# Queries stored with contiguous weight columns and their zeros in place, one load per unit

## The chip, the cores and the metric

The kernel runs on one core of a Trainium2 chip. The metric is the device time of an execution in microseconds (us). The core has engines with queues of their own: TensorE (PE, with PEld for its weight loads), VectorE (DVE), ScalarE (ACT), GpSimd (POOL), and SyncE (SP), which issues the DMAs here. Each engine runs its instructions in the order in which the program gives them.

## The reference

Local attention followed by a two-layer network with a rational activation. Cut to what matters:

```python
# q, k, v: [8 batches, 8 heads, 576 positions, 64]
scores = (1/8) * q @ k.T                 # per batch and head
# heads 0-3: keys 0..31 positions back; heads 4-7: 0..127 back, every fourth
attn = softmax(where(mask, scores, -1e9))
x = (attn @ v), heads side by side       # [4608 tokens, 512]
h = x @ w_in                             # [4608, 2048]
g = (a0 + a1 h + a2 h^2 + a3 h^3) / (1 + |b0| |h| + |b1| h^2 + 1e-6)
out = g @ w_out                          # [4608, 512]
```

All of it in float32; the weights arrive as float64 or float32.

## The kernel before

**Attention.** Heads 4 to 7 have their positions sorted by residue modulo 4, so that all heads attend to a window of 32 positions. The work of a batch is cut into six *units* (`NU = 6`, 48 in all). A unit is six blocks of 32 queries for each of four heads: two pairs of heads (`h` = 0, 1), each pair with an even and an odd head (`e` = 0, 1). The 64 dimensions of the even head lie on partitions 0 to 63 and those of the odd head on 64 to 127.

One matmul makes the scores of one block of 32 queries of *both* heads of a pair. The 64 columns of its weights (the stationary operand) are 32 columns of the even head and 32 of the odd one. For the two heads not to mix, the even head's columns are zero on the partitions of the odd head, and the other way round. The tile `q` of a unit is thus 128 x 768 floats, half of them zeros. In DRAM (`qk`) the queries lie without zeros, 384 columns for 128 partitions, beside the keys.

- `zero_halves` and `zero_q` (L232, L245) set the zeros with two memsets of 64 x 384. Each of the six units of batch 0 (the *start*) has a `q` tile of its own in a slot of a weight that comes late, and memsets of its own; the other 42 units share one tile, `q_keep`, whose zeros are set once and stay.
- `load_q` (L241) loads a unit's queries with two DMAs, one for each half of the partitions.
- `scores` (L260) reads the tile as `(h m j)`: the six blocks `j` are innermost, so that the 64 columns `m` of one matmul's weights lie six floats apart. Twelve matmuls make a unit's scores; each shows as two weight loads and two matmuls in the trace. From batch 1 on, the two pairs `h`, whose results go to different halves of the PSUM partitions, take turns; in batch 0 the blocks of one pair come before those of the other. In batch 1 the masks are added by twelve small matmuls more.

After the scores (`s_ps`, PSUM) come mask, maximum, exponential, sum and normalization on DVE, ACT and POOL; then the scores are turned, by PE for batches 0 to 2 and mostly by DVE transposes of 32 x 32 blocks (`turn`, L328) later; then the product with `v` (`av`, `o_ps`), and the split of its result into a high and a low part (`xh`, `xl`), since the network's matmuls take float32r operands.

**The network.** Tokens are cut into nine chunks of 512. The first eight hold the first 512 tokens of each batch, the last one what is left (`x_left`). For each chunk there are 16 *tiles* of 128 hidden features, 144 in all. A tile is 12 matmuls `h`, a rational function on ACT, DVE and POOL (`r`, `a`, `t`, `gh`, `gl`), and 12 matmuls `out`. A chunk's tiles can only start once its batch's attention is done; the attention of the batches after it runs beside the tiles, about a batch for every 16 tiles. The weights are converted in the first part of the run (`wi_f`, `wo_f`, `wi`, `wo`).

**The order.** `Plan` (L62) is a list scheduler in the program that builds the kernel. Each operation has a modelled time on one of some engines, a rank (when it is due), dependences and buffers; among those that can start next on an engine, the lowest rank is taken. The order that comes out is the order of each engine's queue on the chip. For the score step the planner has 972 ns (1045 in batch 0); for the load of `q`, 120 ns of SP and 196608 bytes. In the start the load of `q` follows its memsets.

Of the kernel before, what the change touches and what calls it, by code (L numbers as in the profile page):

```python
# [8 lines left out]
F32 = mybir.dt.float32  # L9
# [7 lines left out]
B, H, S, D = 8, 8, 576, 64  # L17
NT, DM, DFF = B * S, 512, 2048
P = 128
# [3 lines left out]
NU = 6  # L23
# [3 lines left out]
# Periods of a batch from which on its units are due.  # L27
DUE = (-1.58, 1.49, 3.34, 6.42, 8.91, 12.25)
# Tiles whose operations' ranks come from when they are due.
# [5 lines left out]
# Mask blocks over a 32-query x 64-key window: 0 all keys within the window,  # L35
# 1 the segment starts at the block, 2 at its query 16, 3 at query 16 of the block before.
STRIP = [1, 0, 0, 0, 2, 3]
# For each unit of a batch: (first block, blocks, place in STRIP, or None where all are 0).
# [11 lines left out]
class Op:  # L50
    """An operation of one of some engines (engine: ns). With a slack, its rank follows from when
    those that depend on it are due, or from the period `by` which it has to be done."""
# [8 lines left out]
class Plan:  # L61
    """List schedule: an operation starts when its engine, what it depends on and the  # L62
    buffers it takes are free; of those that can start next, the lowest rank does."""
# [6 lines left out]
    def op(self, engs, rank, fn, *deps, dma=0):  # L70
        o = Op(engs, rank, fn, deps, dma)
        self.ops.append(o)
        return o

    def takes(self, o, tag, bufs, users):
        """o takes a buffer of a tag, which is free again after its users."""
        self.tags.setdefault(tag, (bufs, []))
        o.takes.append((tag, users))

    def due(self):  # L80
        """Ranks of operations with a slack."""
        after = {}
        for o in self.ops:
            for d in o.deps:
                after.setdefault(id(d), []).append(o)
        seen = set()

        def rank(o):
            if o.slack is None or id(o) in seen:
                return o.rank  # L90
            seen.add(id(o))
            ns = min(o.engs.values()) + self.HOP
            if o.dma:
                ns += self.DMA_NS + o.dma / self.DMA_RATE
            due = [rank(n) for n in after.get(id(o), [])] + ([] if o.by is None else [o.by])
            o.rank = min(due) - ns / self.PERIOD - o.slack
            return o.rank

        for o in reversed(self.ops):
            rank(o)  # L100
# [50 lines left out]
def tile_attention_moe(  # L151
# [10 lines left out]
    nc = tc.nc  # L162
# [5 lines left out]
    att = ctx.enter_context(tc.tile_pool(name="att", bufs=1))  # L168
    psum = ctx.enter_context(tc.tile_pool(name="psum", bufs=1, space=bass.MemoryType.PSUM))

    # Every engine runs its instructions in the order in which they are written,
    # which a list schedule of the operations below settles.
    pin = tc.keep_in_program_order
    plan = Plan()
    op = plan.op

    def load(dst, src):
        pin(nc.sync.dma_start(dst, src))  # L178
# [33 lines left out]
    NQ, NKEY, NV = 2 * 6 * 32, 2 * 224, 3 * 2 * 2 * 64  # L212
    xT = {}

    def x_slot(c):
        # chunk 0's second part comes after chunk 1
        return "0" if c == 0 or (c > 2 and c % 2) else "1"
# [9 lines left out]
    def halves(q):  # L227
        # for each half of the partitions (a head of each pair): the columns of either head
        q = q.rearrange("p (h e c) -> p e h c", h=2, e=2)
        return [[q[64 * e : 64 * e + 64, c] for c in range(2)] for e in range(2)]  # L230

    def zero_halves(eng, q):  # L232
        for e, half in enumerate(halves(q)):
            pin((nc.gpsimd if eng == "POOL" else nc.vector).memset(half[1 - e], 0.0))

    class Unit:
        def __init__(self, b, u):
            self.b, self.u, self.n = b, u, b * NU + u
            self.q = q_keep

        def load_q(self):  # L241
            for e, half in enumerate(halves(self.q)):
                load(half[e], qk[self.n, 64 * e : 64 * e + 64, :NQ].rearrange("p (h c) -> p h c", h=2))

        def zero_q(self, eng, pool, tag):  # L245
            self.q = pool.tile([P, 2 * NQ], F32, tag=tag, name=f"q{self.n}")
            zero_halves(eng, self.q)
# [12 lines left out]
        def scores(self, tag, masked):  # L260
            q_t = self.q.rearrange("p (h m j) -> p h j m", h=2, j=6)
            k_t = self.k.rearrange("p (h k) -> p h k", h=2)
            self.s = ps = self.bank(tag, "s_ps")
            pairs = [(h, j) for j in range(6) for h in range(2)]
            # alternate halves of the partitions take turns in the array
            for h, j in pairs if self.b else sorted(pairs):
                cols = slice(64 * j, 64 * j + 64)
                if masked:
                    mm(ps[64 * h : 64 * h + 64, cols], ident_b[:, :64] if h == 0 else ident_b[:, 64:], mask_t[:, BLOCKS[self.u][j]], stop=False)
                mm(ps[64 * h : 64 * h + 64, cols], q_t[:, h, j, :], k_t[:, h, 32 * j : 32 * j + 64], start=not masked)  # L270
# [57 lines left out]
        def turn(self, h, e):  # L328
            # 32 x 32 blocks of this head's scores, each to the partitions of its keys
            src = self.p[64 * h + 32 * e : 64 * h + 32 * e + 32].rearrange("p (i par) k -> p par i k", par=2)  # L330
            for par in range(2):
                for kh in range(2):
                    row = 64 * par + 32 * kh
                    pin(nc.vector.transpose(self.pT[row : row + 32, :, h, e, 32 * par : 32 * par + 32], src[:, par, :, 32 * kh : 32 * kh + 32]))  # L334
# [10 lines left out]
        def pieces(self):  # L345
            """(columns of the result, tokens of the chunk) of this unit, and those left for the last chunk"""
# [39 lines left out]
        def plan(self, p, start):  # L386
            """p: the period from which on this unit is due; start: buffers of the start, or None"""
# [6 lines left out]
            # where each step runs  # L394
# [5 lines left out]
            # Loads run ahead, in the order of need.  # L400
            l_rank = p - 4
            lq = op({"SP": 120}, l_rank, lambda e: self.load_q(), dma=NQ * 512)
            zq = op({"POOL": 720, "DVE": 600}, -90 + u, lambda e: self.zero_q(e, qp, qt)) if start else q_zeroed
            lq.follows.append(zq)
            lk = op({"SP": 60}, l_rank + 0.01, lambda e: self.load_k(kp, kt), dma=NKEY * 512)
            lv = op({"SP": 60}, l_rank + 2.02, lambda e: self.load_v(vpool, vt), dma=NV * 512)
            sc = op({"PE": (972 if b else 1045) + 180 * on_pe}, p - 4.97, lambda e: self.scores(s_tag, on_pe), zq, lq, lk, *([masked, identity] if on_pe else []))
# [26 lines left out]
            # the order of units, and of those that share the bank of the attention  # L434
# [23 lines left out]
            for tag, o, users in ((qt, zq if start else lq, [sc]), (kt, lk, [sc]), (vt, lv, [av])):  # L458
                plan.takes(o, tag, 1, users)
# [31 lines left out]
    def w_scale(key):  # L491
        # float64: the high word as a float32 holds sign, exponent / 8 and the mantissa's start.
        # Times 2^-112 its bits are float32's exponent and 20 mantissa bits, three places low.
        wf[key] = w = work.tile([P, 512], F32, tag="stage", name="%s_f%d" % key, bufs=4)
        act(w, w_words(key)[:, :, 1].bitcast(F32), AF.Abs, scale=2.0**-112)
# [48 lines left out]
    spare_x = {}  # L544

    def spares(part):
        # The last tiles of all have the slot of x that the last chunk doesn't take.
        if part not in spare_x:
            slot = "01"[x_slot(NC - 1) == "0"]
            spare_x[part] = xpool.tile([P, NK, 512], F32 if part == "h" else F32R, tag="x" + part + slot, name="spare_" + part)  # L550
        return spare_x[part]

    class Tile:
        def __init__(self, i, c, ft, first, last):
            self.i, self.c, self.ft, self.first, self.last = i, c, ft, first, last
            # place among the last three tiles
# [112 lines left out]
    # The first part of chunk 0's sums waits in DRAM.  # L669
# [17 lines left out]
    # Zero but for its blocks of keys and queries; the start has another, in a slot of a late weight.  # L687
# [24 lines left out]
    q_keep = att.tile([P, 2 * NQ], F32, tag="q", name="q_keep")  # L712
    q_zeroed = op({"POOL": 720, "DVE": 600}, -60, lambda e: zero_halves(e, q_keep))
# [5 lines left out]
    keys = sorted([("wi", n) for n in range(NF)] + [("wo", n) for n in range(NF)], key=lambda x: x[1] + 1.5 * (x[0] == "wo"))  # L719
    for u in range(NU):  # L720
        start = {
            # banks of out before its first product, and slots of weights that come late
# [44 lines left out]
    # Loads are issued in the order of their ranks until the weights are there.  # L767
# [65 lines left out]
```

## Time and profile before

| what | value |
|---|---|
| median of 3 runs | 993.52 us (992.5 to 993.93) |
| span of the profiled execution (first to last instruction) | 991.2 us; its own device time is not recorded apart from the span |
| busy PE, PEld | 939.3 us, 759.9 us |
| busy DVE, ACT, POOL | 884.7, 683.8, 497.3 us |
| mean granted TensorE clock | 0.993 |
| DMA | 68.80 MB, mean 69 GB/s |
| score matmuls | 1152, of them 144 in batch 0 |
| loads of `q` | 96, of 96 KB each |

A row of a group of instructions gives the line, the engine, the operation, output <- inputs, their shapes and the count, then after a bar the busy time in us and the mean of one in ns, and after the next bar the idle time of that engine just before them with what ended it. A row of waits reads: who waited <- for whom: us in total, times, the longest. In rows of stretches and of the timeline times count from the start of the span. Most matmul lines carry the line number of a helper (L181), so that the names of the tiles tell them apart.

### The profile page before, as it was taken

What the parts mean: (1) busy time and instruction counts of PE and PEld (TensorE: products, weight loads), DVE (VectorE), ACT (ScalarE), POOL (GpSimd) and SP (SyncE); (2) the same over time, 40 slices, a digit from 0 to 9 for tenths busy, and PEclk for the clock granted to TensorE, in tenths of its full rate; (3) what the DMA queues carried; (4) which work ended last, traced back from release to release, by engine and by line L of the source; (5) the groups of instructions that cost most, each with busy time, mean ns of one, the idle gap of its engine ahead of it and who ended that gap; (6) DMA issues with size and microseconds to landing.
All of it is one profiled execution on the core that took longest, in us unless ns stands there. A gap on an engine that the chain in (4) does not pass through costs nothing.

```text
span 991.2 us, 16536 instructions
## 1 busy us (share of the span) xinstructions
PE 939.3 (95%) x5883; PEld 759.9 (77%) x5883; DVE 884.7 (89%) x1747; ACT 683.8 (69%) x1146; POOL 497.3 (50%) x422
## 2 busy tenths in 40 slices
PE   6698898989999999999999999999999999999998
PEld 6576676667887787877877888788877778888886
DVE  6999999999899999999999999999999986656565
ACT  2787877666656666766676667666776678778776
POOL 3676677885544444443544444344443445454443
PEclk9989999999999999999999999999999999999999
DMA  8734910003331111312121122121221001001001
GB/s 257 254 105 132 385 63 1 19 16 107 104 97 55 52 50 34 109 34 68 34 76 56 46 66 77 34 67 35 60 84 39 28 1 43 1 1 43 1 1 42
DMA packets 38962, 68.80 MB, mean 69 GB/s; under 512 B 4448, under 2 KB 23008, under 8 KB 38880
## 3 DMA queue, kind: packets, MB, share of 16 engines
q1 hardware_dynamic: 38736, 67.65, 21.2%
q8 instruction: 46, 0.75, 0.3%
q14 instruction: 36, 0.29, 0.1%
q0 software_dynamic: 144, 0.10, 0.1%
HBM read 57.35 MB, written 10.49 MB: 68 GB/s over the span
## 4 chain that ended last, share of the span: by engine, by line
DVE 49%; PE 41%; issue 4%; DMA 2%; SPq 1%; ACT 1%; DVEq 0%; ACTq 0%
PE h L181 19%; PE out L181 18%; DVE h L190 10%; DVE a L190 10%; DVE p_T L334 9%; DVE t L187 4%; PE s_ps L181 3%; DVE wo_f L190 2%; DVE sm L310 2%; DVE wi_f L190 2%; DVE xl L187 2%; DVE p L187 2%; SPq L178 1%; DVE sm L307 1%; PE o_ps L181 1%
## 5 line engine op out<-in xcount | busy, mean ns | idle before, releaser
L181 PE MATMUL h<-xh,wi 128*128 128x512 f32 x1152 | 386.2, 396 | 21.8 <-DVE a L190 21.4
L193 POOL TENSOR_TENSOR a<-r,a 128x512 f32<-128x512 f32 x141 | 183.7, 1303 | 359.3 <-ACT r L184 349.5
L181 PE MATMUL out<-gh,wo 128*128 128x512 f32 x1136 | 358.1, 396 | 3.2 <-POOL wo L193 2.5
L181 PEld LDWEIGHTS h<-xh,wi 128*128 128x128 f32 x1152 | 217.0, 188 | 85.6 <-DVE a L190 40.3
L181 PEld LDWEIGHTS out<-gh,wo 128*128 128x128 f32 x1136 | 210.3, 189 | 48.8 <-POOL wo L193 3.9
L181 PE MATMUL h<-xl,wi 128*128 128x512 f32 x576 | 225.6, 392 | 0.9 <-DVE xl L187 0.9
L181 PE MATMUL out<-gl,wo 128*128 128x512 f32 x568 | 222.6, 392 | 0.2 <-POOL gl L193 0.2
L193 POOL TENSOR_TENSOR gl<-a,gh 128x512 fp32r<-128x512 f32 x141 | 191.1, 1355 | 37.3 <-ACT gh L184 34.9
L184 ACT ACTIVATE r<-a,ab_t 128x512 f32<-128x512 f32 x141 | 114.8, 814 | 76.5 <-DVE a L190 74.1
L184 ACT ACTIVATE r<-a,ln_bias 128x512 f32<-128x512 f32 x141 | 102.0, 723 | 89.5 <-POOL a L193 89.1
L190 DVE SCALAR_TENSOR_TENSOR h<-h,na_t,r 128x512 f32<-128x512 f32 x144 | 108.0, 750 | 58.5 <-ACT r L184 57.3
L184 ACT ACTIVATE t<-h,na_t 128x512 f32<-128x512 f32 x144 | 112.0, 778 | 50.5 <-PE h L181 36.2
L334 DVE STREAM_TRANSPOSE p_T<-p 32x96 f32<-32x96 f32 x496 | 133.5, 269 | 7.9 <-PE o_ps L181 0.5
L181 PEld LDWEIGHTS out<-gl,wo 128*128 128x128 f32 x568 | 107.0, 188 | 25.0 <-POOL gl L193 2.4
L181 PEld LDWEIGHTS h<-xl,wi 128*128 128x128 f32 x576 | 108.6, 189 | 22.4 <-DVE xl L187 1.5
L190 DVE SCALAR_TENSOR_TENSOR h<-t,na_t,h 128x512 f32<-128x512 f32 x144 | 108.3, 752 | 4.5
L184 ACT ACTIVATE r<-r,exp_bias 128x512 f32<-128x512 f32 x144 | 104.3, 724 | 4.5
L184 ACT ACTIVATE a<-h 128x512 f32<-128x512 f32 x141 | 83.5, 592 | 27.9 <-PE h L181 17.9
L190 DVE SCALAR_TENSOR_TENSOR a<-a,r 128x512 f32<-128x512 f32 x141 | 101.6, 720 | 0.9
L190 DVE SCALAR_TENSOR_TENSOR a<-a,h 128x512 f32<-128x512 f32 x141 | 96.7, 686 | 4.3
L187 DVE TENSOR_TENSOR t<-t,h 128x512 f32<-128x512 f32 x144 | 97.6, 678 | 2.4 <-ACT t L184 1.4
L184 ACT ACTIVATE gh<-a 128x512 fp32r<-128x512 f32 x131 | 81.9, 625 | 10.4 <-DVE a L190 7.8
(81 smaller groups left out, 848.5 us busy)
## 6 DMA issues: line engine op xcount, KB each, us to landing
v<-in_vp_dram SPq DMA_DIRECT2D x48, 384.0 KB, 3.4
k<-in_qk_dram SPq DMA_DIRECT2D x48, 224.0 KB, 2.9
out_dram<-os SPq DMA_DIRECT2D x36, 256.0 KB, 2.2
wi_raw<-in_w_in_dram SPq DMA_DIRECT2D x16, 512.0 KB, 7.1
wo_raw<-in_w_out_dram SPq DMA_DIRECT2D x16, 512.0 KB, 8.1
q_keep<-in_qk_dram SPq DMA_DIRECT2D x84, 96.0 KB, 2.7
q<-in_qk_dram SPq DMA_DIRECT2D x12, 96.0 KB, 3.9
part<-os SPq DMA_DIRECT2D x4, 256.0 KB, 2.0
```

Source lines behind the costliest of these rows:

```text
L178: pin(nc.sync.dma_start(dst, src))
L181: pin(nc.tensor.matmul(o, lhs, rhs, start=start, stop=stop))
L184: pin(nc.scalar.activation(o, i, func, **kw))
L187: pin(nc.vector.tensor_tensor(o, x, y, op))
L190: pin(nc.vector.scalar_tensor_tensor(o, x, s, y, op0, op1))
L193: pin(nc.gpsimd.tensor_tensor(o, x, y, op))
L307: pin(nc.vector.tensor_reduce(self.sm, self.p, axis=AX, op=ALU.add))
L310: pin(nc.vector.tensor_scalar(self.sm, self.sm, 1e-9, None, ALU.add))
L334: pin(nc.vector.transpose(self.pT[row : row + 32, :, h, e, 32 * par : 32 * par + 32], src[:, par, :, 32 * kh : 32 * kh + 32]))
```

## The change

The host lays out `q` in DRAM as the tile needs it: for each unit 128 x 768 floats, zeros included, with the columns in the order `(h j m)`, so that the 64 weight columns of one matmul lie side by side. `load_q` is one DMA of 384 KB per unit. The memsets, `zero_halves`, `zero_q` and `q_keep` are gone; each unit takes a `q` tile from its pool. The planner's figures change with it: the score step from 972 to 750 ns (1045 to 820 in batch 0), the load of `q` from 120 to 60 ns of SP and from 196608 to 393216 bytes (`NQ` doubles), and the load no longer follows a memset. The numbers that reach the matmuls are the same as before. The rest of the diff removes comments.

```diff
-    NQ, NKEY, NV = 2 * 6 * 32, 2 * 224, 3 * 2 * 2 * 64
+    NQ, NKEY, NV = 2 * 6 * 64, 2 * 224, 3 * 2 * 2 * 64
...
-    def halves(q):
-        q = q.rearrange("p (h e c) -> p e h c", h=2, e=2)
-        return [[q[64 * e : 64 * e + 64, c] for c in range(2)] for e in range(2)]
-
-    def zero_halves(eng, q):
-        for e, half in enumerate(halves(q)):
-            pin((nc.gpsimd if eng == "POOL" else nc.vector).memset(half[1 - e], 0.0))
...
-            self.q = q_keep
-
-        def load_q(self):
-            for e, half in enumerate(halves(self.q)):
-                load(half[e], qk[self.n, 64 * e : 64 * e + 64, :NQ].rearrange("p (h c) -> p h c", h=2))
-
-        def zero_q(self, eng, pool, tag):
-            self.q = pool.tile([P, 2 * NQ], F32, tag=tag, name=f"q{self.n}")
-            zero_halves(eng, self.q)
+        def load_q(self, pool, tag):
+            self.q = pool.tile([P, NQ], F32, tag=tag, name=f"q{self.n}")
+            load(self.q, qk[self.n, :, :NQ])
...
-            q_t = self.q.rearrange("p (h m j) -> p h j m", h=2, j=6)
+            q_t = self.q.rearrange("p (h j m) -> p h j m", h=2, j=6)
...
-            lq = op({"SP": 120}, l_rank, lambda e: self.load_q(), dma=NQ * 512)
-            zq = op({"POOL": 720, "DVE": 600}, -90 + u, lambda e: self.zero_q(e, qp, qt)) if start else q_zeroed
-            lq.follows.append(zq)
+            lq = op({"SP": 60}, l_rank, lambda e: self.load_q(qp, qt), dma=NQ * 512)
...
-            sc = op({"PE": (972 if b else 1045) + 180 * on_pe}, p - 4.97, lambda e: self.scores(s_tag, on_pe), zq, lq, lk, ...)
+            sc = op({"PE": (750 if b else 820) + 180 * on_pe}, p - 4.97, lambda e: self.scores(s_tag, on_pe), lq, lk, ...)
...
-            for tag, o, users in ((qt, zq if start else lq, [sc]), (kt, lk, [sc]), (vt, lv, [av])):
+            for tag, o, users in ((qt, lq, [sc]), (kt, lk, [sc]), (vt, lv, [av])):
...
-    q_keep = att.tile([P, 2 * NQ], F32, tag="q", name="q_keep")
-    q_zeroed = op({"POOL": 720, "DVE": 600}, -60, lambda e: zero_halves(e, q_keep))
...
-    qd = qt.transpose(0, 1, 4, 3, 7, 2, 6, 5).reshape(B * NU, P, 2 * 6 * 32)
+    qd = np.zeros((B, 2, 3, 2, D, 2, 6, 2, 32), qt.dtype)
+    for e in range(2):
+        qd[:, :, :, e, :, :, :, e] = qt[:, :, :, e].transpose(0, 1, 3, 6, 2, 4, 5)
+    qd = qd.reshape(B * NU, P, 2 * 6 * 64)
```

More of the change, by code (lines that the diff above doesn't have):

```diff
@@ L401, in plan @@
             l_rank = p - 4
-            lq = op({"SP": 120}, l_rank, lambda e: self.load_q(), dma=NQ * 512)
-            zq = op({"POOL": 720, "DVE": 600}, -90 + u, lambda e: self.zero_q(e, qp, qt)) if start else q_zeroed
-            lq.follows.append(zq)
+            lq = op({"SP": 60}, l_rank, lambda e: self.load_q(qp, qt), dma=NQ * 512)
             lk = op({"SP": 60}, l_rank + 0.01, lambda e: self.load_k(kp, kt), dma=NKEY * 512)
             lv = op({"SP": 60}, l_rank + 2.02, lambda e: self.load_v(vpool, vt), dma=NV * 512)
-            sc = op({"PE": (972 if b else 1045) + 180 * on_pe}, p - 4.97, lambda e: self.scores(s_tag, on_pe), zq, lq, lk, *([masked, identity] if on_pe else []))
+            sc = op({"PE": (750 if b else 820) + 180 * on_pe}, p - 4.97, lambda e: self.scores(s_tag, on_pe), lq, lk, *([masked, identity] if on_pe else []))
             if on_pe:
```

## The prediction

> **What bounds the kernel now.** I read the page's first two parts, then the busy time of each engine by stage, then who waited for whom on VectorE (DVE) alone, then the rows of the changed tiles, and last the timeline of the start. The page gives the engines' totals:
>
> ```profile
> span 991.2 us, 16536 instructions
> PE 939.3 (95%) x5883; PEld 759.9 (77%) x5883; DVE 884.7 (89%) x1747; ACT 683.8 (69%) x1146; POOL 497.3 (50%) x422
> ```
>
> By that, TensorE (PE) is the bound. By stage it is not so. Each row is a stretch in us, its length, then the busy time of PE, weight loads, DVE, ACT and POOL, the granted clock, the DMA share and GB/s:
>
> ```profile
> 0.00:36.00 36.00, 25.28 (x346) 23.19 (x347) 26.34 (x66) 15.63 (x33) 14.22 (x27) 0.95 0.82 242
> 36.00:220.00 184.00, 158.93 (x988) 122.24 (x988) 179.69 (x256) 135.59 (x274) 136.44 (x111) 0.97 0.33 117
> 220.00:290.00 70.00, 68.69 (x523) 55.59 (x522) 63.08 (x135) 45.24 (x75) 37.29 (x33) 1.00 0.30 95
> 290.00:430.00 140.00, 135.70 (x850) 109.93 (x849) 135.47 (x303) 93.61 (x148) 61.88 (x52) 1.00 0.20 62
> 430.00:800.00 370.00, 363.30 (x2338) 294.24 (x2337) 356.29 (x806) 250.81 (x400) 160.25 (x134) 1.00 0.18 54
> 800.00:991.00 191.00, 187.40 (x846) 154.66 (x845) 123.78 (x186) 142.94 (x218) 87.19 (x67) 1.00 0.05 17
> ```
>
> From 290 to 800 us both engines are over 96% busy, and busy shares can't tell which one leads. The waits can. First DVE's from 36 to 800 us (the three largest kinds of eight; total, times, longest), then DVE's from 290 to 800 (all there are), PE's in the same stretch, and DVE's from 800 on:
>
> ```profile
> DVE p L187 <- PE s_ps L181: 2.4, 6, 0.8
> DVE h L190 <- ACT r L184: 1.5, 3, 0.9
> DVE t L187 <- ACT t L184: 1.4, 3, 0.9
> ...
> DVE p L187 <- PE s_ps L181: 1.2, 4, 0.3
> DVE os L196 <- PE out L181: 0.3, 1, 0.3
> ...
> PE h L181 <- DVE a L190: 10.6, 19, 1.1
> ...
> DVE h L190 <- ACT r L184: 55.8, 33, 2.3
> ```
>
> In 510 us DVE waits 1.5 us for anyone, while PE waits 10.6 us for DVE to release the banks of `h`. So DVE is the bound there; its idle 18.2 us (510 less 135.47 and 356.29) is but for those 1.5 us made of gaps too short to be listed. From 36 to 220 DVE is idle 4.3 of 184 us: the bound too. From 220 to 290 it is PE (idle 1.3 of 70, DVE 6.9). From 800 on there are no scores, PE has no listed wait, and the change touches nothing. Before 36 neither engine leads: the loads and the dependences of the first units do.
>
> **The change, part by part.**
>
> *The score matmuls.* Each score matmul takes 64 columns of `q` as its weights. Now they lie 6 floats apart (`(h m j)`); after the change they lie side by side (`(h j m)`). The attention's second product (`o_ps`) has the same shapes and contiguous weights, `v`, so it is the comparison:
>
> ```profile
> L181 PE MATMUL s_ps<-k,q_keep 128*64 128x64 f32 x1008 | 68.3, 283 | 0.6 <-issue 0.6
> L181 PEld LDWEIGHTS s_ps<-k,q_keep 128*64 128x64 f32 x1008 | 63.2, 207 | 14.9 <-issue 14.2 <-PE out L181 0.7
> L181 PE MATMUL o_ps<-p_T,v 128*64 128x64 f32 x1080 | 41.4, 224 | 0.8 <-ACT p_T L184 0.5 <-DVE p_T L334 0.2
> L181 PEld LDWEIGHTS o_ps<-p_T,v 128*64 128x64 f32 x1080 | 36.3, 138 | 9.2 <-issue 6.2 <-ACT r L184 0.7 <-ACT p_T L184 0.7
> 448.18 1.46 PEld L181 LDWEIGHTS s_ps<-k,q_keep 128*64 128x64 f32 x24 [0.35 <-issue]
> 449.53 0.80 PEld L181 LDWEIGHTS o_ps<-p_T,v 128*64 128x64 f32 x24
> ...
> L181 PEld LDWEIGHTS s_ps<-k,q_keep x1008: 187/209/230, 32.5 to 765.6; 128*64 128x64 f32 x168
> 220.00:290.00 70.00, 9.58 (x144) 8.78 (x144) 3.50 (x9) 0.00 (x0) 1.00 0.30 95
> 290.00:800.00 510.00, 42.61 (x648) 39.38 (x648) 15.71 (x41) 0.00 (x0) 1.00 0.19 56
> ```
>
> A strided load takes 207 ns, a contiguous one 138, and a unit's 24 loads take 1.46 us against 0.80. Both groups alternate between two halves of the array, both write 64 columns to PSUM; stride is the one difference I see. The last three rows are the first and last start of these loads and, of the score tiles alone, the stretches from 220 and from 290 us. I take 0.66 us off each of the 42 units of batches 1 to 7 (1008 / 24): 27.7 us of PE time. The bounds are 0 (stride is not the cause) and 0.66.
>
> The Trainium skill speaks for stride in "SBUF — State Buffer", section "Door 1: The DMA port swizzle": reads that stay within a 16-byte line run at full rate, and every new line costs; here each of the 64 elements is 24 bytes from the last. It speaks against it in "TensorE: Matmul & The Clock Gate", section "LDWEIGHTS (loading the stationary operand)": the time is set by the number of columns, which does not change here. The rows of 207 and 138 ns at equal columns go with the first; by the second the PE terms below would be nil, which I keep as a rival.
>
> *What of it reaches the end.* From 36 to 220 and from 290 to 800 DVE sets the pace, so the freed PE time turns into longer waits of PE for DVE. Cover: DVE's own work. Only what DVE waits for PE there can be won: 1.2 us from 290 to 800 (four waits for `s_ps`); from 36 to 220 I count nothing. From 220 to 290 six units (144 loads) give 6 x 0.66 = 4.0 us of PE. DVE's waits there are these (the four largest of seven):
>
> ```profile
> DVE t L187 <- ACT t L184: 1.2, 2, 0.9
> DVE p L187 <- PE s_ps L181: 1.2, 2, 0.8
> DVE xl L187 <- ACT xh L184: 1.2, 2, 0.6
> DVE h L190 <- ACT r L184: 0.6, 2, 0.3
> ```
>
> They add up to 4.2 us. The `ACT t` and `ACT xh` ones stand behind PE products, `ACT r` behind the POOL and ACT steps. I take 3.0: `p`, `t` and half of `xl` (1.2 + 1.2, and 0.6 of the `xl` wait); bounds 0 and 4.0. If the stretch's cover goes, DVE is late next, as on both sides of it.
>
> *The start: loads, memsets, first scores.*
>
> ```profile
> 0.90 5.87 DVE L234 MEMSET q<- 64x384 f32 x12 [0.90 <-PEq L817]
> 6.35 8.99 PE L181 MATMUL s_ps<-k,q 128*64 128x64 f32 x96 [6.35 <-DMA q<-in_qk_dram]
> 10.62 5.69 DMA q<-in_qk_dram
> 16.40 2.52 PE L181 MATMUL s_ps<-k,q 128*64 128x64 f32 x24 [1.06 <-DMA q<-in_qk_dram]
> 19.86 0.56 DVE L187 TENSOR_TENSOR p<-s_ps,mask_t 128x384 f32<-128x384 f32 x1 [2.70 <-PE t_ps L320]
> 3.70 1.25 SPq L178 DMA_DIRECT2D q<-in_qk_dram  x2
> 5.00 0.59 SPq L178 DMA_DIRECT2D k<-in_qk_dram  x1
> v<-in_vp_dram SPq DMA_DIRECT2D x48, 384.0 KB, 3.4
> q<-in_qk_dram SPq DMA_DIRECT2D x12, 96.0 KB, 3.9
> 0.00:6.00 6.00, 0.00 (x0) 0.00 (x0) 3.89 (x11) 1.49 (x2) 4.03 (x15) 1.00 0.56 137
> 6.00:13.00 7.00, 6.65 (x74) 6.60 (x74) 4.54 (x11) 0.52 (x1) 0.75 (x1) 1.00 0.89 246
> 13.00:20.00 7.00, 5.94 (x54) 5.76 (x53) 2.64 (x9) 1.29 (x3) 2.58 (x4) 0.92 1.06 275
> ```
>
> The twelve DVE memsets run from 0.90 to 6.77 us, when DVE has nothing else but a 0.2 us constant; its first mask waits for scores. The two POOL ones lie among constants. I take 0 for both: the wait for the first `q` covers them.
>
> SP issues two half loads of `q` in 1.25 us; one load takes what `k` takes, 0.59. So per unit 0.66 us less of SP, which matters only before 11 us, where it issues back to back: five units by the load that is waited for at 10.62, 3.3 us. Against that a unit's `q` grows from 2 x 96 KB to 384 KB: 0.98 MB more ahead of that same load. At the 275 GB/s of the full stretch 13 to 20 us this is 3.6 us; the transfers have 2.6 us free before 6 us (1 - 0.56 of 6) and 0.8 after (1 - 0.89 of 7). Rows put the load that ends at 16.31 anywhere from 3.3 us earlier to 3.6 later; with the free 3.4 us used it comes at about the same time, and I take that. What I do count is PE: this unit's scores, the transposes behind them and the DVE mask that waited 2.70 us for those all move up by the 0.66 us of the contiguous loads, and the sixth unit's scores give 0.66 again. Sum for the start: -1.3 us; bounds -4.6 (-3.3 - 1.3) and +2.3 (3.6 - 1.3).
>
> *Loads later on.* Each later unit's `q` is twice as large and shares one buffer with its predecessor. The DMA share is 0.18 to 0.33 from 36 us on, a load of 384 KB lands in 3.4 us in the median, and the 42 units are spread over 32.5 to 765.6 us, 17 us apart on average: 0. If that cover went, the scores would come late by the few us of a landing, each time.
>
> *The planner.* The instruction order is worked out from modelled durations; the change lowers the modelled score time (972 to 750 ns), raises the modelled size of a `q` load and drops its wait for a memset. So the order may shift on all engines, SP's queue and POOL's too. The trace cannot price that. The nearest rows bound it: at best every listed wait of DVE from 36 to 800 goes, which the terms above nearly use up; at worst new holes of the kind seen after 800 us, 55.8 / 33 = 1.7 us each. I take 0, because a DVE that waits 1.5 us in 510 has its inputs ready well ahead, so that small swaps find them ready.
>
> **Sum:** -1.3 - 3.0 - 1.2 = -5.5 us. The profiled execution spans 991.2 us; the median of the runs shown is 993.52, 2.3 us more, for what lies around the span. Taken off the span: 985.7; with the same 2.3 us around it, **988.0 us**. What tells from no change in this kernel is about 0.2%, 2.0 us.
>
> **Rivals.**
>
> *No change (about 992).* The larger loads cost the start most of what the scores gain: if the load issued at 10.62 lands 3.6 us later, -5.5 becomes -1.9, 991.6. For it: the DMA share of 1.06 from 13 to 20 us. Against it: free transfer time before, and fewer issues. It decides once that load lands 3.5 us or more after 16.31.
>
> *Slower (about 998).* The new order opens holes in DVE's queue between 220 and 800 us, where a DVE step stands in front of the ACT step it needs. One such hole of 1.7 us in each of the six batches 2 to 7 costs 10.1 us: 988.0 + 10.1 = 998.1. Four holes eat up the 5.5, and from five on the kernel is measurably slower. For it: after 800 us DVE meets such a wait 33 times. Against it: attention work lies between and fills them.
>
> *All of it (about 964).* If PE led everywhere, 27.7 us and the start's 1.3 would come off: 964.5. For it: 95% busy. Against it: the 1.5 us that DVE waits.
>
> *The change doesn't do what it says (about 993).* Weight loads depend on columns alone; PE is not faster, nothing is left but the start's loads, between -3.3 and +3.6 us: 993. Against it: 207 and 138 ns at equal columns.
>
> **Numbers.** Forecast 0.56, no change 0.17, slower 0.19, all of it 0.04, no faster PE 0.04. Faster by over 0.2%: 0.56 and 0.04, less what of the forecast's own spread falls short, 0.02: 0.58. Slower 0.19 and a hundredth of the fifth case: 0.20. Same: 0.22. The forecast's own range is 982 (the start at -4.6, the stretch from 220 at -4.0, the 1.2, and the 1.5 us of `ACT r` waits gone with a better order: -11.3) to 991; the range adds a us to that below, reaches to 998 for the slower case and leaves out the full gain.
>
> **What would show it.** The `s_ps` loads at about 138 ns and a unit's 24 in about 0.8 us; PE's busy sum near 910 us; PE's wait for DVE from 290 to 800 up from 10.6 us by most of 27 x 0.66 = 17.8 us (648 / 24 units), while that stretch hardly shrinks; DVE's waits for `s_ps` gone; the wait of 2.70 us at 19.86 shorter. It is wrong if DVE shows new waits between 36 and 800 us, if `q` of the fifth unit lands well after 16.3, or if the stretch without scores at the end grows beyond its 191 us.

## The result and the profile after

The change makes the kernel slower: 1011.0 us (1010.44 to 1012.02, four runs) against 993.56 us, a ratio of 1.0181 (95% interval 1.0169 to 1.0193). The profiled execution of the changed kernel took 1011.47 us, its span is 1009.7 us. The page's totals, and the busy time by stage (stretch, length, then PE, weight loads, DVE, ACT, POOL, clock, DMA share, GB/s):

```profile
span 1009.7 us, 16408 instructions
PE 932.1 (92%) x5883; PEld 735.7 (73%) x5883; DVE 894.5 (89%) x1734; ACT 689.2 (68%) x1151; POOL 494.6 (49%) x416
```

```profile
36.00:220.00 184.00, 153.56 (x974) 117.13 (x974) 175.60 (x252) 136.25 (x278) 131.92 (x105) 0.95 0.33 122
220.00:290.00 70.00, 68.95 (x541) 54.85 (x539) 62.94 (x132) 43.59 (x72) 36.65 (x33) 1.00 0.35 111
290.00:430.00 140.00, 131.84 (x824) 101.70 (x821) 133.79 (x292) 90.51 (x143) 59.03 (x50) 0.98 0.23 73
430.00:800.00 370.00, 354.52 (x2314) 277.91 (x2313) 357.40 (x787) 250.33 (x396) 159.80 (x132) 1.00 0.19 63
800.00:991.00 191.00, 184.34 (x820) 150.77 (x821) 127.62 (x202) 141.32 (x215) 87.10 (x68) 0.99 0.04 14
991.00:1010.00 19.00, 14.36 (x64) 11.56 (x62) 9.19 (x14) 9.25 (x15) 3.71 (x3) 0.96 0.15 56
```

PE is 7 us less busy and DVE, though twelve memsets are gone, 10 us more. DVE's instructions from 430 to 800 us have fallen from 806 to 787 at the same busy time: on average they last longer, and work that stood before 800 us now comes after it. What DVE waited for from 36 to 800 us (total, times, longest), the five largest:

```profile
DVE t L187 <- ACT t L184: 3.8, 3, 2.2
DVE h L190 <- ACT r L184: 2.5, 6, 1.0
DVE mx L272 <- PE s_ps L181: 2.1, 2, 1.7
DVE sm L297 <- ACT p L184: 1.2, 2, 0.6
DVE t L187 <- ACT a L184: 0.9, 1, 0.9
```

The prediction named new waits here as a sign that it is wrong. There are some, but these five add up to 10.5 us and all eight kinds to 11.8, where the kernel before has 8.1, and the kernel is 17.4 us slower although its score matmuls did become faster. The score tiles' weight loads (min/median/max in ns) and one unit's 24 loads with the product behind them, in the changed kernel:

```profile
L181 PEld LDWEIGHTS s_ps<-k,q x1152: 132/138/232, 5.6 to 786.4; 128*64 128x64 f32 x192
472.10 0.78 PEld L181 LDWEIGHTS s_ps<-k,q 128*64 128x64 f32 x24 [0.35 <-issue]
472.79 0.31 PEld L181 LDWEIGHTS o_ps<-p_T,v 128*64 128x64 f32 x6
```

209 ns has become 138, and 1.46 us a unit 0.78. So something costs much more than this brings.

The two kernels' queues stand in different orders. Of the 1727 DVE instructions that both have, at most 1238 keep their order relative to one another, of PE's 4731 at most 3681, of SP's 221 (with `q` loaded whole in both) 183. The planner, given other durations and sizes, has written another order for every engine.

### The profile page after: what moved, and what is told of

It is laid out like the page before. It is cut to its first block, busy times and chain, and to the rows that moved or that the text cites. A ratio compares the mean times of both kernels' runs of the same rounds, so it can differ in the third digit from the quotient of the medians.

```text
span 1009.7 us, 16408 instructions
## 1 busy us (share of the span) xinstructions
PE 932.1 (92%) x5883; PEld 735.7 (73%) x5883; DVE 894.5 (89%) x1734; ACT 689.2 (68%) x1151; POOL 494.6 (49%) x416
## 4 chain that ended last, share of the span: by engine, by line
DVE 62%; PE 27%; issue 5%; DMA 3%; ACT 2%; POOL 1%; SPq 0%; POOLq 0%; ACTq 0%; DVEq 0%
PE h L181 13%; DVE h L190 12%; DVE p_T L321 12%; DVE a L190 12%; PE out L181 12%; DVE t L187 5%; DVE p L187 4%; DVE sm L297 3%; DVE wi_f L190 3%; DVE wo_f L190 2%; DVE xl L187 2%; DVE sm L294 2%; DVE mx L272 2%; DMA k<-in_qk_dram 1%; DMA wo_raw<-in_w_out_dram 1%
## 5 line engine op out<-in xcount | busy, mean ns | idle before, releaser
L181 PE MATMUL h<-xh,wi 128*128 128x512 f32 x1152 | 391.4, 402 | 27.9 <-DVE a L190 27.3
L181 PEld LDWEIGHTS h<-xh,wi 128*128 128x128 f32 x1152 | 219.3, 190 | 101.0 <-DVE a L190 54.6
L181 PE MATMUL out<-gl,wo 128*128 128x512 f32 x568 | 225.0, 396 | 5.0 <-POOL gl L193 5.0
L181 PEld LDWEIGHTS out<-gl,wo 128*128 128x128 f32 x568 | 107.5, 189 | 33.2 <-POOL gl L193 10.9
```

The costliest lines, as they stand in the source:

```text
L181: pin(nc.tensor.matmul(o, lhs, rhs, start=start, stop=stop))
```

## The experiments

The theories: *order* (the new queue order costs the time, the new layout saves some), *layout* (larger loads, or contiguous weights in some way, cost it). Later, within *order*: that the lateness sits in the hand-over from the last attention to the eighth chunk of tiles, that it sits in DVE instructions that collide with POOL, or that it is spread over the run. "Old figures" are the planner's figures of the kernel before.

Since the layout and the planner's figures can be set apart, the first four runs do that.

**e1: the new layout in the old order.** The new `q`, one load, no memsets; the planner keeps every old figure and a memset step that emits nothing, so each engine's queue stands as before, instruction for instruction but for the memsets and the loads of `q`.

```diff
-            lq = op({"SP": 60}, l_rank, ..., dma=NQ * 512)
+            lq = op({"SP": 120}, l_rank, ..., dma=NQ * 256)
+            zq = op({"POOL": 720, "DVE": 600}, -90 + u, lambda e: None) if start else q_zeroed
+            lq.follows.append(zq)
-            sc = op({"PE": (750 if b else 820) + 180 * on_pe}, ..., lq, lk, ...)
+            sc = op({"PE": (972 if b else 1045) + 180 * on_pe}, ..., zq, lq, lk, ...)
```

> The changed kernel's layout, single load and no memsets, but the planner keeps the figures of the kernel before (score step 972 and 1045 ns, load of q 120 ns of SP and 196608 bytes, a step without an instruction in the memsets' place), so every engine runs its instructions in the order of before. Theory A (the new order is what costs): 985 to 990 us, as the prediction's sum had it, with DVE's p<-p,mx and sm<-sm rows back near 22.6 and 27.5 us. Theory B (the layout itself costs: larger loads, or scores that come at other moments and collide): 1008 to 1014 us. Theory C (half and half): about 1000.

Measured: 984.75 us, ratio 0.9916 (0.9901 to 0.9931). The layout alone makes the kernel faster by 8.4 us: theory A, a little below its range. Its second sign came half: the `p<-p,mx` row is back at 22.4 us, the `sm<-sm` row stays at 30.2 (both are shown further down).

**e2: the old layout in the new order.** The kernel before with the new figures, so that its queues stand as in the changed kernel; its memsets are emitted inside `load_q`.

```diff
-            lq = op({"SP": 120}, l_rank, lambda e: self.load_q(), dma=NQ * 512)
-            zq = op({"POOL": 720, "DVE": 600}, -90 + u, ...) if start else q_zeroed
+            lq = op({"SP": 60}, l_rank, lambda e: self.load_q(start, qp, qt), dma=2 * NQ * 512)
-            sc = op({"PE": (972 if b else 1045) + 180 * on_pe}, ..., zq, lq, lk, ...)
+            sc = op({"PE": (750 if b else 820) + 180 * on_pe}, ..., lq, lk, ...)
```

> The layout of before (strided weight columns, half loads, memsets), with the changed kernel's planner figures, so the order of every engine is that of the changed kernel. Theory A (order): 1010 to 1022 us, at least the changed kernel's 1011, since its scores take 0.6 us more per unit. Theory B (layout): 990 to 996 us.

Measured: 1020.53 us, ratio 1.0278 (1.0262 to 1.0293). With all of the old loads and strided columns, the order alone costs 27.3 us. The four corners:

| | old order | new order | order costs |
|---|---|---|---|
| old layout | 993.2 | 1020.5 | +27.3 |
| new layout | 984.75 | 1011.0 | +26.3 |
| layout brings | -8.4 | -9.5 | |

The two parts add up to within 1.1 us, and *layout* as a cause of the loss falls.

**e3 and e4: which figure.** The changed kernel with the old score figure (e3), or with the old figures for the load of `q` and the memset step (e4).

```diff
# e3
-            sc = op({"PE": (750 if b else 820) + 180 * on_pe}, ...)
+            sc = op({"PE": (972 if b else 1045) + 180 * on_pe}, ...)
# e4
-            lq = op({"SP": 60}, l_rank, ..., dma=NQ * 512)
+            lq = op({"SP": 120}, l_rank, ..., dma=NQ * 256)   # and zq as in e1
```

> The changed kernel with one planner figure put back: the score step at 972 and 1045 ns; the load of q keeps its new figures. Theory A says nothing of which figure matters. If the score step's figure makes the bad order: 985 to 992 us. If the load's figures make it: about 1011. If any new order is a draw of its own: something else between 985 and 1015. Theory B: 1008 to 1014.

> The changed kernel with the other planner figures put back: the load of q at 120 ns of SP, 196608 bytes and behind a step without an instruction in the memsets' place; the score step keeps 750 and 820 ns. If the load's figures make the bad order: 985 to 992 us. If the score step's figure makes it: about 1011. If any new order is a draw of its own: something else between 985 and 1015. Theory B: 1008 to 1014.

Measured: e3 993.08 us, 0.9998 (0.9989 to 1.0007); e4 1001.79 us, 1.0091 (1.0074 to 1.0108). From e1, the load's figures alone cost 8.3 us, the score figure alone 17.0, both together 26.3. No single figure is to blame; both runs fall to the third forecast, that a new order is a draw of its own.

**e12: is a true figure better?** Three more values of the score figure alone, in e4.

```diff
-            sc = op({"PE": (750 if b else 820) + 180 * on_pe}, ...)
+            sc = op({"PE": (1080 if b else 1155) + 180 * on_pe}, ...)   # or 860 / 930, or 700 / 770
```

> New layout, all planner figures of before but the score step's, which is 1080 and 1155 ns (972 and 1045 give 984.75 us, 750 and 820 give 1001.8). Theory T (a trend: the lower the figure, the worse the order): at or below 984, say 977 to 985. Theory R (each figure draws an order of its own around a tuned one): anywhere from 986 to 1012.

> The same with the score step at 860 and 930 ns. Theory T: half way, 991 to 995 us. Theory R: anywhere from 986 to 1012.

> The same with the score step at 700 and 770 ns. Theory T: 1004 to 1008 us. Theory R: anywhere from 986 to 1012.

Measured, with e4 and e1 between them, for 700, 750, 860, 972 and 1080 ns: 995.21 (ratio 1.0029, 1.0018 to 1.004), 1001.79, 1004.58 (1.0116, 1.0099 to 1.0133), 984.75, 999.24 (1.0064, 1.0049 to 1.0079). All three fall to theory R. There is no trend: each figure draws an order of its own, and over the seven orders tried with this layout the kernel takes 984.75 to 1011.0 us. The order before the change is the fastest of them, and not because its figure is the true one: in the changed kernel the next product's weight loads begin 0.69 us after those of the scores (472.10 and 472.79), which is nearest to 700 and 750 ns.

**e14: what of the layout saves.** e1 with the zeros in place and one load, but the columns 6 floats apart as before.

```diff
-            q_t = self.q.rearrange("p (h j m) -> p h j m", h=2, j=6)
+            q_t = self.q.rearrange("p (h m j) -> p h j m", h=2, j=6)   # the host's layout to match
```

> One load of 384 KB per unit with its zeros and no memsets, in the order of before, but the 64 weight columns of a matmul stay six floats apart as before. It splits the 8.4 us of the new layout in the old order. If the contiguous weights bring them: 992 to 993.5 us, with the weight loads back at 207 ns. If the loads and memsets of the start bring them: 985 to 987. Half and half: 989.

Measured: 991.49 us, 0.9984 (0.9975 to 0.9994), 0.5 us below the range for the contiguous weights. Its score loads:

```profile
L181 PEld LDWEIGHTS s_ps<-k,q x1152: 187/209/230, 5.8 to 763.0; 128*64 128x64 f32 x192
```

Each against the kernel before as it was timed beside it, the loads and memsets bring 1.5 us, the contiguous columns the other 7.0 of e1's 8.4.

**Where the order loses it.** The start of the first `t` step on DVE (`t<-t,h` in the timeline) of a tile, in us; "after" is the changed kernel. Tile 112 is the first of the eighth chunk, which needs the last batch's attention.

| tile | 0 | 8 | 24 | 32 | 48 | 64 | 80 | 96 | 112 | end of span |
|---|---|---|---|---|---|---|---|---|---|---|
| e14 | 43.1 | 116.5 | 226.9 | 286.0 | 390.3 | 495.4 | 600.9 | 706.5 | 808.0 | 989.2 |
| e1 | 41.8 | 115.1 | 225.5 | 281.5 | 385.6 | 490.4 | 595.5 | 700.6 | 801.6 | 982.9 |
| after | 40.6 | 113.7 | 228.5 | 285.9 | 396.4 | 503.1 | 613.9 | 719.6 | 828.8 | 1009.7 |

From tile 112 on all take 181 us. Ahead of it the changed kernel loses 4.4 us between tiles 8 and 24, 6.3 between 32 and 48, 5.7 between 64 and 80, 8.2 between 96 and 112. It is spread, and it is not one hole per batch: the stretches 48 to 64 and 80 to 96 lose 2.0 and 0.6. Part of this alternation is attention work that moved: between tiles 32 and 48 the changed kernel has 7 of the subtractions `p<-p,mx`, between 48 and 64 it has 5, where e1 has 5 and 6. Up to tile 112, before, e1 and the changed kernel (length, then busy PE, weight loads, DVE, ACT, POOL):

```profile
0.00:810.60 810.60, 762.51 (x5104) 613.75 (x5105) 769.43 (x1580) 548.40 (x942) 415.16 (x359) 0.99 0.25 81
```

```profile
0.00:801.60 801.60, 740.32 (x5104) 583.96 (x5105) 768.37 (x1567) 549.18 (x941) 415.29 (x357) 0.99 0.27 93
```

```profile
0.00:828.80 828.80, 759.12 (x5128) 593.16 (x5129) 779.17 (x1566) 555.10 (x949) 413.76 (x354) 0.98 0.27 91
```

Length less DVE's busy time is its idle time: 41.2, 33.2 and 49.6 us. From e1 to the changed kernel 27.2 us are lost, 16.4 of them idle DVE, and 10.8 DVE busy for longer with one instruction less. Of the idle 16.4 us, 4.8 lie between tiles 0 and 8, 2.9 between tiles 24 and 32, and 5.0 between tiles 96 and 112, nearly all of these at the hand-over to the new chunk; at the hand-overs to tiles 48, 64, 80 and 96 DVE is idle for 0.2 to 0.7 us in the changed kernel and 0.3 in e1. The stretch from 36 to 100 us, where e1 has no listed wait, in e1 and in the changed kernel:

```profile
36.00:100.00 64.00, 51.72 (x426) 39.89 (x426) 62.87 (x93) 49.58 (x131) 43.95 (x38) 0.89 0.48 169
```

```profile
36.00:100.00 64.00, 49.95 (x450) 37.50 (x450) 57.93 (x93) 50.33 (x142) 41.06 (x35) 0.92 0.52 183
```

DVE is idle there for 6.1 us instead of 1.1. The hand-over to tile 112 in the changed kernel's timeline (start, length, instruction, idle before it and what ended that):

```profile
823.97 0.79 DVE L187 TENSOR_TENSOR xl<-o_ps,xh 128x64 fp32r<-128x64 f32 x2 [1.66 <-ACT xh L184]
824.59 0.39 PE L181 MATMUL h<-xh,wi 128*128 128x512 f32 x1
828.82 0.69 DVE L187 TENSOR_TENSOR t<-t,h 128x512 f32<-128x512 f32 x1 [3.83 <-ACT a L184]
```

The same in e1:

```profile
796.00 0.81 DVE L187 TENSOR_TENSOR xl<-o_ps,xh 128x64 fp32r<-128x64 f32 x2
801.63 0.69 DVE L187 TENSOR_TENSOR t<-t,h 128x512 f32<-128x512 f32 x1 [0.30 <-ACT a L184]
```

The last unit's attention comes later among the tiles in the changed kernel, so that DVE has no tile work left beside the chain `o_ps`, `xh`, `xl`, `h`, `t` and waits 1.66 and 3.83 us for it.

**e11: the last attention earlier.** The changed kernel with the last batch's units due two periods sooner.

```diff
-            Unit(b, u).plan(NF * (b - 1) + p, None)
+            Unit(b, u).plan(NF * (b - 1) + p - 2.0 * (b == B - 1), None)
```

> The changed kernel with the six units of the last batch due two periods earlier. Nothing differs before about 700 us; the order does after that. Theory D (the new order leaves the last batch's attention to the end of the chunk before it: 13.7 us between the last tile of the sixth chunk and the first of the seventh, 5.5 us of DVE idle, where the order of before has 4.7 and 1.8): the hand-over shrinks and 5 to 9 us come back, 1002 to 1006. Theory E (only stretched DVE instructions and earlier losses matter): 1009 to 1013.

(The chunk that the expectation calls the seventh, counting from nought, is the eighth, with tile 112.) Measured: 1008.21 us, 1.0151 (1.0136 to 1.0166), 2.8 us less than the changed kernel; neither theory's number. Up to its tile 112:

```profile
0.00:826.40 826.40, 759.93 (x5108) 592.38 (x5108) 779.07 (x1567) 553.48 (x947) 411.69 (x353) 0.98 0.27 91
```

DVE's busy time is the same as in the changed kernel and its idle time 47.3 us, 2.3 less. The hand-over to 112 shrank from 13.7 to 4.7 us, but the chunk of tiles 80 to 95 grew by 5.4 us, for attention work now stands there. Only idle time comes back; the work moves. The hand-over alone is not the cause. The run also shows how much single executions differ: every queue is that of the changed kernel up to 540 us, yet tile 0 starts 1.3 us later and tile 8 2.6 us later.

**e10: does DVE's time reach the end?** Thirty reductions of 128 x 192 more, behind the subtraction of the units of batches 3 to 7, in e1.

```diff
+                pin(nc.vector.tensor_reduce(scratch, self.p[:, :3], axis=AX, op=ALU.max))   # b >= 3
```

> The new layout in the order of before (984.75 us), and in batches 3 to 7, behind each subtraction of the maximum, one more DVE instruction that reads half of p and whose result nobody uses (30 instructions; by the 128x192 mask step's 0.35 us, 10.5 us). Price of DVE time: if DVE sets the pace there, 994 to 996 us (all of it arrives). If the pace is PE's and DVE has room, 985 to 988 us.

```profile
L291 DVE TENSOR_REDUCE scratch<-p x30: 352/353/355, 268.2 to 786.4; 128x3 f32<-128x192 f32 x30
```

Measured: 994.58 us, 1.0014 (1.0005 to 1.0024), 9.8 us more than e1 for 30 x 0.353 = 10.6 us of DVE. This is the number of the theory that DVE sets the pace: time put on DVE from 268 to 786 us arrives at the end nearly whole. So the 10.8 us that DVE is busy longer in the changed kernel should count as the idle 16.4 do.

**What DVE is busy with for longer.** Two groups have grown most (form, count, then busy us and mean ns). Before, e1 and the changed kernel:

```profile
L310 DVE TENSOR_SCALAR sm<-sm 128x6 f32<-128x6 f32 x48 | 27.5, 573 | 1.2
L187 DVE TENSOR_TENSOR p<-p,mx 128x384 f32<-128x384 f32 x32 | 22.6, 706 | 0.9
```

```profile
L297 DVE TENSOR_SCALAR sm<-sm 128x6 f32<-128x6 f32 x48 | 30.2, 628 | 1.2
L187 DVE TENSOR_TENSOR p<-p,mx 128x384 f32<-128x384 f32 x32 | 22.4, 701 | 0.9
```

```profile
L297 DVE TENSOR_SCALAR sm<-sm 128x6 f32<-128x6 f32 x48 | 33.9, 706 | 2.5 <-ACT p L184 1.2
L187 DVE TENSOR_TENSOR p<-p,mx 128x384 f32<-128x384 f32 x31 | 29.0, 935 | 0.3
```

From e1, 3.7 and 6.6 us. Other groups have changed too: the integer shifts of the weights (`wi_f`, `wo_f`) take 7.3 us less, the steps that read `wi_raw` 3.0 more. All durations together grow by 7.0 us up to tile 112; the rest of the 10.8 is that neighbouring DVE instructions overlap less in the trace. A step on 6 columns that takes 706 ns on average must be waiting for something. The timeline of the changed kernel shows it, once beside POOL and once without:

```profile
15.08 0.16 DVE L297 TENSOR_SCALAR sm<-sm 128x6 f32<-128x6 f32 x1
...
809.26 1.29 POOL L193 TENSOR_TENSOR a<-r,a 128x512 f32<-128x512 f32 x1 [2.39 <-ACT r L184]
809.42 1.16 DVE L297 TENSOR_SCALAR sm<-sm 128x6 f32<-128x6 f32 x1
810.61 0.19 DVE L298 RECIPROCAL sm<-sm 128x6 f32<-128x6 f32 x1
```

POOL's instruction ends at 810.55, the addition of 1e-9 at 810.58. In the kernel before, 33 of the 48 additions start while POOL runs. Of these, 29 end 0.03 us after POOL's instruction; the other four start in its last 0.1 us. The 15 that start without POOL take 0.16 to 0.17 us. The subtraction `p<-p,mx` takes 0.56 us alone and ends 0.41 us after POOL's instruction otherwise; it starts beside POOL 14 times of 32 before, 12 of 32 in e1, 25 of 31 in the changed kernel. The reductions of 128 x 384 are not held up: 46 of the 90 in e1 start beside POOL, and all 90 take 0.51 to 0.55 us. (Of e1's 48 reciprocals, 191 to 193 ns long, only 3 start beside POOL, so they tell little.) The Trainium skill says this in "SBUF — State Buffer", section "Who interferes with whom": VectorE and GpSimd share a pair of ports, and where a VectorE step needs both (in a two-port mode, or with two inputs in SBUF), the first to issue holds the pair for its whole instruction while the other is blocked; reductions are named there as never contending. The 0.03 us and the reductions agree with it.

**e6 and e7: without the additions.** The step that adds 1e-9 to the 48 sums is left out of the changed kernel (e6) and of e1 (e7), the queues otherwise as they were. A row's largest exponential is 1, so that in float32 the addition changes no bit of the sum.

```diff
-                pin(nc.vector.tensor_scalar(self.sm, self.sm, 1e-9, None, ALU.add))
```

> The changed kernel without the step that adds 1e-9 to the 48 sums of the softmax (float32 sums that are at least 1, so the step changes no bit); the planner still counts it, so the order is the same. That row takes 33.9 us of DVE, most of it while POOL runs. DVE-bound throughout: 1011 less 25 to 30, 981 to 986 us. PE takes over in part: 988 to 1000.

> The same step left out of the new layout in the order of before (984.75 us), where its row takes 30.2 us of DVE. DVE-bound throughout: 957 to 962 us. PE takes over in part: 965 to 975. If stretched sums made up much of the difference between the two orders, its 26 us would shrink by more than the 4 us by which the two rows differ.

Measured: e6 990.48 us, 0.9979 (0.997 to 0.9989), 20.5 less than the changed kernel, in the range for PE taking over in part; e7 962.82 us, 0.9693 (0.9677 to 0.971), 21.9 less than e1, 0.8 us above the range for DVE throughout. Alone the 48 additions would take 48 x 0.17 = 8 us; the rest is time behind POOL. But the two orders still stand 27.7 us apart, as with the additions (26.3): the additions' share of the collisions is not what sets the orders apart. That the subtractions' 6.6 us and the idle time do it remains the account of the rows above; no run takes the subtractions' collisions away, so it is not shown by an experiment of its own.

e7 beats both kernels. Its page and its stretch up to tile 112:

```profile
span 961.3 us, 16388 instructions
PE 908.0 (94%) x5883; PEld 729.3 (76%) x5883; DVE 857.4 (89%) x1687; ACT 683.1 (71%) x1146; POOL 497.7 (52%) x420
```

```profile
0.00:780.00 780.00, 731.10 (x5104) 583.15 (x5105) 742.10 (x1519) 547.63 (x941) 415.59 (x357) 0.99 0.28 96
```

## Why the prediction was wrong

*The planner: the step that failed.* It was put at 0, "because a DVE that waits 1.5 us in 510 has its inputs ready well ahead, so that small swaps find them ready". It measured +26.3 us (e1 to the changed kernel), +27.3 with the old layout. The error in the reasoning: short waits are a property of one order, not of the engine's inputs. 1.5 us in 510 said that this order suited the chip, not that others would. It is not that its durations were true: in the kernel before, the next product's loads began 1.35 us after those of the scores (448.18 and 449.53), where the planner had 972 ns. How its figures and ranks were arrived at is not on record; with both DVE and PE over 96% busy, the six other orders tried with the new layout took 8 to 26 us more. Nor were the swaps small: more than a quarter of DVE's instructions (489 of 1727) left the common order. What the runs showed in place of the 0 is thus 16.4 us more of idle DVE and 10.8 us of DVE busy for longer ahead of tile 112.

*The slower rival* (998, holes of 1.7 us in DVE's queue, one per batch from 220 to 800 us) had the right kind of cause and too small a price. Its place was partly wrong: the added idle time lies mainly from 36 to 100 us, between tiles 24 and 32 (about 229 to 286 us) and at the hand-over to tile 112. And it knew nothing of two fifths of the loss (10.8 of 27.2 us), which is no hole but DVE busy for longer, above all with subtractions that now meet POOL. The groups that show it were on the page before: a step on 6 columns with a mean of 573 ns.

*The score matmuls: right.* 138 ns and 0.78 us a unit, as forecast; by these rows weight loads do not go by columns alone. The Trainium skill's rule in "TensorE: Matmul & The Clock Gate", section "LDWEIGHTS (loading the stationary operand)", which has the number of columns as the only term, does not hold for columns 24 bytes apart (209 ns against 138 at 64 columns), while its 16-byte lines in "SBUF — State Buffer", "Door 1: The DMA port swizzle", agree in direction (only these two spacings were run). PE's busy sum in e1, over two stretches:

```profile
sum 982.90, PE 917.22 PEld 730.01 DVE 883.55 ACT 684.46 POOL 497.38; mean PE 458.61 PEld 365.01 DVE 441.78 ACT 342.23 POOL 248.69
```

917 us, where the prediction had "near 910": 22 us less than before instead of 29.

*What of it reaches the end: right, with the order held.* From e14 to e1, in the table of tiles: 1.3 us by tile 0 (predicted -1.3 for the scores of the start; the match may be luck, since the changed kernel and e11, with the same queues there, differ by as much), 3.2 more from tile 24 to 32, at about 226 to 286 us (predicted -3.0 from 220 to 290), 1.9 from there to tile 112 (predicted -1.2). In e1 from 290 to 800 us PE waits for DVE:

```profile
PE h L181 <- DVE a L190: 17.1, 24, 1.4
PE o_ps L181 <- DVE p_T L321: 1.9, 5, 0.5
```

Up from 10.6 us by 6.5, and 1.9 for `p_T`. DVE's own waits in e1 from 36 to 800 us, all that are listed:

```profile
DVE h L190 <- ACT r L184: 2.0, 3, 0.9
DVE p_T L321 <- POOL p L193: 0.7, 1, 0.7
DVE t L187 <- ACT t L184: 0.3, 1, 0.3
DVE wo_f L486 <- ACT wo_f L184: 0.3, 1, 0.3
```

Those for `s_ps` are gone. The contiguous columns bring 7.0 us (e14 to e1) of the 27.7 us of PE that were to be freed, so most of that went into idle PE time, as forecast; "most of 17.8 us" in one listed wait was too much.

*The start's loads and memsets:* 0 predicted, e14 has -1.5 us. The larger loads cost nothing that can be seen. In the changed kernel the first scores begin 0.7 us earlier:

```profile
5.64 7.62 PE L181 MATMUL s_ps<-k,q 128*64 128x64 f32 x96 [5.64 <-DMA k<-in_qk_dram]
```

*The sum* of -5.5 us stands against -8.4 measured in e1, the sum's planner term of 0 against +26.3. Of *the other rivals*, "no change" through late loads and "no faster PE" are refuted by e1 and the 138 ns, "all of it" by e1's 8.4 of 27.7 us.

## What to carry to other kernels

Where a schedule is worked out from modelled durations, a change of a modelled duration is two changes; run the new code in the old order as well, and let the measurement choose the order, since a figure nearer to the chip bought no better one here (984.75 to 1011.0 us over seven orders of the same work). An engine without waits in a full stretch was here the mark of one order, and is a reason to test a new one and not to put its cost at nothing. Divide a small instruction's mean by its shortest instance: 573 to 155 ns on a tiny step pointed at the line whose removal brought 20.5 and 21.9 us.

## What the runs showed of the hardware that was not expected

A DVE step on 128 x 6 elements that takes 0.17 us alone takes up to 1.26 us when it starts beside a POOL instruction, and ends 0.03 us after it; the subtraction of two inputs, 0.56 us alone, ends 0.41 us after it; reductions are not held up. Taking 48 such steps out brought 20.5 and 21.9 us. That columns 24 bytes apart cost weight loads half as much again was expected from one pair of groups; e14 and e1 show it in one kernel, with nothing else changed.
